# A fused S4D and SwiGLU block on one Trainium2 core: gate and up projections of two token blocks at once by Strassen's scheme

## The chip, the core and the metric

The kernel runs on one NeuronCore of one Trainium2 chip. A core has TensorE (PE, matrix products into PSUM), VectorE (DVE), ScalarE (ACT), GpSimd (POOL) and SyncE (SP), whose queue issues most DMA transfers. The metric is the time of one execution on the device in microseconds, lower is better. Three runs of the kernel before gave 1016.65, 1013.78 and 1016.82 us; the median is 1016.65 us.

## The reference

Input `x` is 2048 tokens of 640 channels. Stage A is a state space convolution, stage B a gated feed-forward layer with a hidden width of 1728:

```python
def _B_ref(x, w1, w3, w2):
    gate = jnp.einsum("bsd,df->bsf", x, w1)
    up = jnp.einsum("bsd,df->bsf", x, w3)
    h = _silu(gate) * up
    out = jnp.einsum("bsf,fd->bsd", h, w2)
    return out
...
h = _layernorm(x, axis=-1) * (1 + ca) + sa
x = x + ga * _A_ref(h, A_log_A_real, A_A_imag, A_C_real, A_C_imag, A_log_dt, A_D_skip)
h = _layernorm(x, axis=-1) * (1 + cb) + sb
x = x + gb * _B_ref(h, B_w1, B_w3, B_w2)
```

The six vectors `sa` to `gb` come from a product of `silu(c)` with `w_mod`. The change is in the second half, the layer norm and `_B_ref`; all operands are float32.

## The kernel before

**Stage A** (up to about 390 us of the span) makes the convolution in five channel blocks of 128 by small products. Its instructions stand in a table of tasks (`Plan`), whose ranks in `RANKS` set the order on every engine; they go through a helper that records them, so most have line 156 in the profile. Its result goes to the DRAM tensor `zd`, from where the last inverse product (`inverse`, matmuls `iy`) reads it row by row as tiles `iz` and adds it to the tokens `x2`. The fifth channel block is finished last, and its part of `zd` is read apart, as `izb`.

**Stage B** (`ffn`) works on four blocks of 512 tokens. A block is normalised (`ln2`): statistics on DVE, `xn` on ACT and DVE, 20 transposes on PE (`tp`), then `v`, split into a high part `xh` and a low part `xl`. Every float32 operand is split so: `split` copies it to a rounded form on ACT (line 658) and subtracts that on DVE (line 659). A float32 product is then three matmuls, high by high, high by low, low by high (lines 769 to 771 in `up`, lines 803 to 805 in `down`).

The hidden width is 13 tiles of 128 and a last one of 64, where gate and up share one tile. For each block and tile, `weights_load` fetches 128 columns of `w1`, `w3` and 128 rows of `w2`, `split` makes `wh`, `wl`, `w2h`, `w2l`; `up` makes gate and up in two PSUM banks with 2 x 5 x 3 = 30 matmuls of 128x512; `gate` makes `a = silu(gate) * up` (tanh on ACT, two operations on DVE) and splits it into `ah` and `al`; `down` adds the tile's part to five banks `acc` with 15 matmuls. `down` of a tile is called behind `up` of the next one, across the border of two blocks too. `output` scales `acc`, transposes it back and adds it to `x2`, which is stored. PSUM holds five `acc` banks and three `gu` banks. The tile framework's scheduler sets the order in stage B, by the program's order and its own estimate.

While block 0 runs, its `mid` reads and inverts rows 4 to 15 of `zd`, two at a time; rows 0 to 3 were done ahead of it. All weights are fetched and split again for each of the four blocks.

Of the kernel before, what the change touches and what calls it, by code (L numbers as in the profile page):

```python
# [18 lines left out]
P = 128  # L19
# [147 lines left out]
class Plan:  # L167
# [7 lines left out]
    def __init__(self, **rings):  # L175
        self.tasks, self.n = {}, rings

    def add(self, name, eng, took, f, after=(), rank=0.0, port=False, take=(), give=(), table=None, dma=None):
        assert name not in self.tasks, name
        take = [(r, name + "".join(x), k) for r, k, *x in take]  # L180
# [86 lines left out]
    def run(self):  # L267
# [3 lines left out]
        assert not found or len(found) == len(T)  # L271
        self.order = self.place(dict(zip(T, found)) if found else {n: t[4] for n, t in T.items()})
# [5 lines left out]
class K:  # L278
# [34 lines left out]
    def rsqrt(self, pool, var, n, tag, mean, scale=1.0, work=None):  # L313
# [3 lines left out]
        y = pool.tile([P, n], F32, name=f"rs_y_{tag}", tag="rs_y")  # L317
        nb = pool.tile([P, n], F32, name=f"rs_n_{tag}", tag="rs_n")
# [16 lines left out]
    def ln_begin(self, pool, tag):  # L335
        return (pool.tile([P, 4, KT, 6], F32, name=f"st_{tag}", tag="ln_st", bufs=1),
                pool.tile([P, 4, 2], F32, name=f"mv_{tag}", tag="ln_mv", bufs=1))
# [302 lines left out]
    def inverse(self, j0, nj, z, ps, tag, bufs, d0, d1):  # L640
        nc = self.nc
        w = d1 - d0
        for j in range(nj):
            for o, n in ((0, w),) if w <= 512 else ((0, 320), (320, 320)):
                py = ps.tile([P, 512], F32, name=f"iy{j0 + j}_{d0 + o}", tag=tag, bufs=bufs)
                for pr in range(2):
                    nc.tensor.matmul(py[pr * 64:(pr + 1) * 64, :n], self.wd[:, j0 + j, pr, :], z[pr][:, j, o:o + n],
# [13 lines left out]
    def ln2(self, b, pool, ps, stats=None, po=None):  # L661

        nc = self.nc
        xs = self.x2[b]
        st, mv = stats or self.ln_begin(pool, f"n{b}")
        for j in range(4):
            self.ln_part(st, xs, j, KT - 1 if stats else 0, KT)
        rstd, nb = self.ln_end(pool, st, mv, f"n{b}")
        xn = pool.tile([P, 4, D], F32, name=f"xn{b}", tag="xn", bufs=1)
        for j in range(4):  # L670
            if j % 2:
                nc.vector.tensor_scalar(xn[:, j, :], xs[:, j, :], rstd[:, j:j + 1], nb[:, j:j + 1], op0=ALU.mult, op1=ALU.add)
            else:
                nc.scalar.activation(xn[:, j, :], xs[:, j, :], AF.Identity, scale=rstd[:, j:j + 1], bias=nb[:, j:j + 1])
        xh = pool.tile([P, KT, 512], F32R, name=f"xh{b}", tag="xh", bufs=2)
        xl = pool.tile([P, KT, 512], F32R, name=f"xl{b}", tag="xl", bufs=2)
# [15 lines left out]
    def weights(self, b, m, wp):  # L692
        return self.weights_load(b, m, wp)()
# [792 lines left out]
```

## Time and profile before

| | us |
|---|---|
| median of three runs | 1016.65 |
| profiled execution, span from first to last instruction | 1015.7 |
| median less that span | 0.95 |
| PE busy in the span | 892.4 |
| DVE, ACT, POOL busy | 655.7, 506.8, 279.5 |

The answers of the trace hold no time of the profiled execution itself beside its span; the 0.95 us are the difference to the median of the other runs. In the profile a matmul's busy time reaches to its modelled end, and the next starts before that, so a group of matmuls shows a mean of 0.39 us where one starts every 0.23 us; how many fall in a stretch tells the rate. "Idle before" is what an engine waited just ahead of a group. Rows that start with SPq are DMA issues of SP's queue.

### The profile page before, as it was taken

The numbers are of one execution on the slowest core, as the hardware profiler recorded it, in microseconds if no ns is written. First come the engines' busy times: TensorE is split into PE (matmuls) and PEld (weight loads), VectorE is DVE, ScalarE is ACT, GpSimd is POOL, SyncE is SP. The second block draws the span as 40 slices with busy tenths as digits, with TensorE's granted clock in tenths as the row PEclk, the third lists the DMA queues.
The fourth block names the chain that finished last, engine by engine and source line by source line (L and its number), as shares of the span: only waits on it lengthen the run. The fifth ranks groups of instructions, "written<-read, shape, count | busy, mean of one in ns | idle before, by whom it ended". The sixth has DMA issues, their size and how long they took to land.

```text
span 1015.7 us, 20252 instructions
## 1 busy us (share of the span) xinstructions
PE 892.4 (88%) x8129; PEld 713.3 (70%) x8129; DVE 655.7 (65%) x1212; ACT 506.8 (50%) x845; POOL 279.5 (28%) x288
## 2 busy tenths in 40 slices
PE   1464878789999884899999999999999999999996
PEld 1133756767887762677788888888888888888884
DVE  7998899989999474677674453463553643534332
ACT  6867788879787540432243342342442432523231
POOL 1798798978998200100000000000000000000000
PEclk9977998989999897899999999999999999999998
DMA  9965453524131759867232353232443323533302
GB/s 216 264 203 165 105 134 104 141 61 109 37 93 47 194 132 238 211 169 170 77 101 81 111 141 112 78 104 78 127 120 109 88 79 100 139 108 91 103 14 53
DMA packets 140998, 122.05 MB, mean 120 GB/s; under 512 B 13416, under 2 KB 124776, under 8 KB 139368
## 3 DMA queue, kind: packets, MB, share of 16 engines
q1 hardware_dynamic: 140360, 120.49, 44.4%
q8 instruction: 64, 1.05, 0.4%
q10 hardware_dynamic: 544, 0.26, 0.1%
q14 instruction: 30, 0.25, 0.1%
HBM read 99.75 MB, written 20.97 MB: 119 GB/s over the span
## 4 chain that ended last, share of the span: by engine, by line
PE 73%; DVE 14%; ACT 4%; issue 3%; DMA 3%; POOL 1%; SPq 1%; ACTq 0%; DVEq 0%
PE gu L770 12%; PE gu L771 12%; PE gu L769 12%; PE acc L803 6%; PE acc L804 6%; PE acc L805 6%; PE ps L156 4%; PE kps L156 3%; DVE yy L156 3%; PE fz L156 3%; PE fk L156 2%; PE fh L156 2%; DVE fp L156 2%; DVE xx L156 2%; DVE hn L156 2%
## 5 line engine op out<-in xcount | busy, mean ns | idle before, releaser
L770 PE MATMUL gu<-xl,wh 128*128 128x512 f32 x540 | 212.1, 393 | 0.0
L771 PE MATMUL gu<-xh,wl 128*128 128x512 f32 x540 | 211.2, 391 | 0.0
L769 PE MATMUL gu<-xh,wh 128*128 128x512 f32 x540 | 210.1, 391 | 0.6 <-ACT xh L658 0.6
L658 ACT ACTIVATE wh<-wr 128x640 fp32r<-128x640 f32 x105 | 71.8, 731 | 137.3 <-PE gu L770 137.3
L726 POOL MEMSET w2l<- 64x640 f32 x3 | 1.9, 629 | 450.4 <-PE acc L804 450.4
L769 PEld LDWEIGHTS gu<-xh,wh 128*128 128x128 f32 x540 | 101.3, 188 | 23.6 <-ACT xh L658 0.8
L770 PEld LDWEIGHTS gu<-xl,wh 128*128 128x128 f32 x540 | 101.5, 188 | 22.1 <-DVE xl L659 0.2
L771 PEld LDWEIGHTS gu<-xh,wl 128*128 128x128 f32 x540 | 101.4, 188 | 21.5
L803 PE MATMUL acc<-ah,w2h 128*128 128x512 f32 x260 | 103.9, 399 | 0.3 <-ACT ah L658 0.3
L804 PE MATMUL acc<-ah,w2l 128*128 128x512 f32 x260 | 102.2, 393 | 0.0
L783 DVE SCALAR_TENSOR_TENSOR a<-th,gu 128x512 f32<-128x512 f32 x52 | 35.8, 688 | 101.2 <-ACT th L782 101.2
L784 DVE TENSOR_TENSOR a<-a,gu 128x512 f32<-128x512 f32 x52 | 35.8, 688 | 99.5 <-PE gu L771 99.5
L782 ACT ACTIVATE th<-gu 128x512 f32<-128x512 f32 x52 | 31.1, 599 | 134.1 <-PE gu L771 134.1
L805 PE MATMUL acc<-al,w2h 128*128 128x512 f32 x260 | 96.5, 392 | 0.0
L156 POOL TENSOR_TENSOR yy<-e,e 128x512 f32<-128x512 f32 x80 | 86.2, 1093 | 19.4 <-PE kps L156 14.6
L659 DVE TENSOR_TENSOR wl<-wr,wh 128x640 fp32r<-128x640 f32 x105 | 82.1, 819 | 10.6 <-ACT wh L658 10.6
L658 ACT ACTIVATE w2h<-w2r 128x640 fp32r<-128x640 f32 x51 | 37.7, 738 | 87.0 <-issue 47.7
L156 POOL TENSOR_TENSOR ph<-p,p 128x1024 int32<-128x1024 int32 x40 | 79.0, 1976 | 7.5 <-ACT tr L156 6.7
L659 DVE TENSOR_TENSOR w2l<-w2r,w2h 128x640 fp32r<-128x640 f32 x51 | 42.0, 824 | 57.7 <-ACT w2h L658 57.4
L156 PE MATMUL kps<-yy,xx 128*32 128x64 f32 x2560 | 51.7, 235 | 30.8 <-DVE xx L156 20.3
L156 DVE TENSOR_TENSOR yy<-yy,tr 128x512 f32<-128x512 f32 (+1 forms) x80 | 75.5, 946 | 0.9 <-ACT tr L156 0.6
L156 PEld LDWEIGHTS kps<-yy,xx 128*32 128x32 f32 x2560 | 45.2, 117 | 40.8 <-issue 24.9
(205 smaller groups left out, 1645.1 us busy)
## 6 DMA issues: line engine op xcount, KB each, us to landing
wr<-in_w SPq DMA_DIRECT2D x104, 320.0 KB, 3.7
w2r<-in_w SPq DMA_DIRECT2D x52, 320.0 KB, 2.9
zd<-zt SPq DMA_DIRECT2D x40, 256.0 KB, 3.0
iz<-zd SPq DMA_DIRECT2D x24, 320.0 KB, 6.9
xs<-in_x SPq DMA_DIRECT2D x16, 320.0 KB, 10.7
hs<-hb SPq DMA_DIRECT2D x20, 256.0 KB, 2.4
xb<-hs SPq DMA_DIRECT2D x20, 256.0 KB, 4.5
x<-in_x SPq DMA_DIRECT2D x16, 320.0 KB, 9.7
```

The lines of the kernel that those rows point to most:

```text
L156: self.prev = self.k.order(f(*a, **kw), self.prev)
L658: self.nc.scalar.activation(H, v, AF.Copy)
L659: eng.tensor_tensor(Lo, v, H.bitcast(F32), op=ALU.subtract)
L769: nc.tensor.matmul(pg, wh[:, k, :], xh[:, k, :], start=(k == 0), stop=False)
L770: nc.tensor.matmul(pg, wh[:, k, :], xl[:, k, :], start=False, stop=False)
L771: nc.tensor.matmul(pg, wl[:, k, :], xh[:, k, :], start=False, stop=(k == KT - 1))
L782: nc.scalar.activation(th, gu[0], AF.Tanh, scale=0.5)
L783: nc.vector.scalar_tensor_tensor(a, th, 1.0, gu[0], op0=ALU.add, op1=ALU.mult)
L784: nc.vector.tensor_mul(a, a, gu[1])
L803: nc.tensor.matmul(acc[k], w2h[:, sl], ah, start=(m == 0), stop=False)
L804: nc.tensor.matmul(acc[k], w2l[:, sl], ah, start=False, stop=False)
L805: nc.tensor.matmul(acc[k], w2h[:, sl], al, start=False, stop=(m == 12))
```

## The change

Token blocks are taken in pairs. For a pair, the contraction over 640 channels is cut in 2 x 256 and a rest of 128. Gate and up by first and second half, times first and second half by two blocks, is a 2x2 by 2x2 product of blocks; `group` makes it with seven products of 128 x 256 x 512 for eight (Winograd's form of Strassen's scheme), each of 2 x 3 matmuls, and adds the rest directly: 7 x 6 + 4 x 3 = 54 matmuls for a tile of a pair. Before, two blocks took 2 x 30.

- `x_sums` makes four sums and differences of the pair's activations (`T1` to `T4`), once for a pair; `factors` makes four of the weights on POOL for each tile; `part(i)` splits the eight operands of the next tile, each into a buffer of its own that is used again right behind the product that read it.
- Bank `x` is read by ACT and then added to, three times a group; ACT copies and DVE adds take the place of direct reads of PSUM.
- Weights `w1` and `w3` are fetched and split for a pair, `w2` for each block.
- The hidden tile of the pair's second block is kept in SBUF (`ha`, `hb`), and its down projection runs behind all the tiles of the pair, in `late`, 205 matmuls in a row. For pair 0, `late` also holds the norm, the transposes and the sums of blocks 2 and 3, and the 64-wide tile of pair 1. For pair 1 the last two tiles go by output column, with `output` between, and the block is stored in two parts.
- Tile 0 and the 64-wide tile of pair 0 and the 64-wide tile of pair 1 go the plain way (`plain`).
- In stage B the matmuls are chained in the order of the program (`InOrder`), so their line is 156.
- Rows 4 to 7 of `zd` and the tokens of block 1 are read ahead of stage B, as four new tasks of the plan with ranks of their own (`own`); rows 8 to 15 are read one at a time in the groups.
- `wd` is four tiles for one, a few small tiles have two buffers, and the descriptor scratch of software DMA is set to 8192 bytes.

```diff
-        def mid(b, m):
-            if b == 0 and m in (1, 3):
-                self.load_x2((m + 3) // 2)
-            if b == 0 and 2 <= m + 1 < 8:
-                self.inverse_unit(m + 1, ip, ps, "gu", 3)
-            if m == 8 and b < 3:
-                nxt[b + 1] = self.ln2(b + 1, pool, ps)
...
-        self.ffn(nxt, wp, pool, ps, po, mid)
...
+    def x_sums(self, X, v, p, i, tag, bufs):
...
+        def one(t, a, b, eng):
+            d = self.tmp(f"{t}{p}{i}", tag, bufs)
+            eng.tensor_tensor(d, a, b, op=ALU.subtract)
+            h, l = X[t]
+            self.split(h[:, i], l[:, i], d, nc.vector)
+            return d
+        t1 = one("T1", v12, v11, nc.vector)
+        t2 = one("T2", v22, t1, nc.vector)
+        one("T4", v21, t2, nc.gpsimd)
+        one("T3", v22, v12, nc.gpsimd)
...
+    def factors(self, p, m, raw):
+
+        nc = self.nc
+        V, G = nc.vector, nc.gpsimd
+        s = [self.fp.tile([P, 2, P], F32, name=f"s{i}{p}_{m}", tag=f"s{i}") for i in range(4)]
+        g, u = raw[:, 0], raw[:, 1]
+
+        def sums():
+            G.tensor_tensor(s[0], u[:, 0:2], u[:, 2:4], op=ALU.add)
+            G.tensor_tensor(s[1], s[0], g[:, 0:2], op=ALU.subtract)
+            G.tensor_tensor(s[2], g[:, 0:2], u[:, 0:2], op=ALU.subtract)
+            G.tensor_tensor(s[3], g[:, 2:4], s[1], op=ALU.subtract)
+        src = {0: g[:, 0:2], 1: g[:, 2:4], 2: s[3], 3: u[:, 2:4], 4: s[0], 5: s[1], 6: s[2], 7: raw[:, :, 4]}
+        W = {}
+
+        def part(i, eng=None):
+            W[i] = self.operand(i, f"{p}{m}", src[i], eng or V)
+        return sums, part, W
...
+    def product(self, out, w, x, start, stop=True):
+        for k in range(2):
+            self.three(out, [t[:, k] for t in w], [t[:, k] for t in x], start and k == 0, stop and k == 1, not start)
+
+    def rest(self, out, W, i, x, more=False):
+        self.three(out, [t[:, i] for t in W[7]], [t[:, 0] for t in x], False, True, more)
...
+    def hidden(self, b, m, th, g, u):
+
+        V, A = self.nc.vector, self.nc.scalar
+        V.scalar_tensor_tensor(g, th, 1.0, g, op0=ALU.add, op1=ALU.mult)
+        if b % 2:
+            h = self.h[m] = self.h_tile(m)
+            V.tensor_mul(h, g, u)
+            return
+        V.tensor_mul(g, g, u)
+        return self.hidden_split(b, m, g, self.nc.vector)
...
+    def group(self, p, m, W, X, step, mid, quick):
...
+        copy = lambda o, i: A.activation(o, i, AF.Copy)
+        tanh = lambda o, i: A.activation(o, i, AF.Tanh, scale=0.5)
+        b11, b21, k40, k41 = X[0, 0], X[0, 1], X[0, 2], X[1, 2]
+        x = self.bank(f"X{n}")
+        self.product(x, W[0], b11, True)
+        g0 = self.tmp(f"g0{n}")
+        copy(g0, x)
+        step(0)
+        c = self.bank(f"c0{n}")
+        self.product(c, W[1], b21, True, False)
+        self.rest(c, W, 0, k40)
+        self.add_(g0, c, g0)
+        t0 = self.tmp(f"t0{n}")
+        tanh(t0, g0)
+        step(1)
+        e = self.bank(f"c1{n}")
+        self.product(e, W[4], X["T1"], True)
+        u1 = self.tmp(f"u1{n}")
+        copy(u1, e)
+        step(4)
+        mid()
+        self.product(x, W[5], X["T2"], False)
+        g1 = self.tmp(f"g1{n}")
+        copy(g1, x)
+        step(5)
+        quick()
+        self.product(e, W[2], X[1, 1], False, False)
+        self.rest(e, W, 0, k41, True)
+        self.add_(g1, e, g1)
+        t1 = self.tmp(f"t1{n}")
+        tanh(t1, g1)
+        step(2)
+        self.product(x, W[6], X["T3"], False)
+        u0 = self.tmp(f"u0{n}")
+        copy(u0, x)
+        step(6)
+        c = self.bank(f"c2{n}")
+        self.product(c, W[3], X["T4"], True, False)
+        self.rest(c, W, 1, k40)
+        self.add_(u0, c, u0)
+        step(3)
+        self.rest(x, W, 1, k41, True)
+        self.add_(u1, x, u1)
+        step(7)
+        a = self.hidden(0, m, t0, g0, u0)
+        self.hidden(1, m, t1, g1, u1)
+        return a
...
+    def ffn(self, cut):
...
+        first, half = self.ahead
+        h0 = self.plain(0, X, [(0, first[0]), (13, half[0])])
+        for b in (2, 3):
+            self.load_x2(b)
+        xn = self.ln_norm(1, *self.ln_stats(1, *self.stats[1], KT - 1))
+        for k in range(KT):
+            v[1, k] = self.tmp(f"v1{k}", "hb", 10)
+            self.turn_x(1, k, xn, X, v[1, k], acc_bank(1, k), k % 2)
+        acc = self.accumulators(0)
+        self.down(acc, 0, h0[0], first[1], True, False)
+        self.plain(1, X, [(0, first[0])])
+        self.down(acc, 13, h0[1], half[1], False, False)
+        raw, w2r = self.up_load(0, 1), self.down_load(0, 1)
+        sums, part, W = self.factors(0, 1, raw)
+        sums()
+        for i in (0, 1, 7, 4, 3):
+            part(i)
+        self.plain(1, X, [(13, half[0])])
+        for i in (5, 2, 6):
+            part(i)
+        for i in range(2):
+            self.x_sums(X, [v[0, i], v[1, i], v[0, 2 + i], v[1, 2 + i]], 0, i, "tmp", 7)
+        w2 = self.down_split(0, 1, w2r)
+        pend = self.groups(0, range(1, 13), X, acc, W, w2, None)
+        acc, X, W, w2, pend = self.late(0, acc, pend)
+        pend = self.groups(1, range(13), X, acc, W, w2, pend)
+        self.late(1, acc, pend)
...
+    def groups(self, p, tiles, X, acc, W, w2, pend):
+
+        for m in tiles:
+            more = m < 12
+            if more:
+                raw, w2r = self.up_load(p, m + 1), self.down_load(2 * p, m + 1)
+                sums, part, W2 = self.factors(p, m + 1, raw)
+                sums()
+            rows = []
+
+            def mid():
+                if pend is not None:
+                    self.down(acc, *pend, False)
+                if p == 0 and m < 9:
+                    rows.append(self.inverse_row(7 + m))
+                    rows[0](0)
+
+            def quick():
+                if rows:
+                    rows[0](320)
+            a = self.group(p, m, W, X, part if more else lambda i: None, mid, quick)
+            pend = (m, a, w2, False)
+            if more:
+                W, w2 = W2, self.down_split(2 * p, m + 1, w2r)
...
+    def late(self, p, acc, pend):
...
+        ready(0)
+        self.down(acc, *pend, True)
+        if p == 0:
+            xn.append(self.ln_norm(2, *self.stats[0]))
+        for k in range(KT):
+            self.output(2 * p, acc, k)
+        self.store(2 * p)
+        acc = self.accumulators(b)
+        for i, m in enumerate(self.H[:n - self.LAST] if p else self.H):
+            a = self.hidden_split(b, m, self.h.pop(m), nc.gpsimd if i % 2 == 0 else nc.vector)
+            self.down(acc, m, a, w2.pop(i), i == 0, i == n - 1)
+            ready(i + 1)
...
+            if i in (6, 8):
+                for k in (0, 2) if i == 6 else (1, 3, 4):
+                    v[1, k] = self.tmp(f"v3{k}", "hb", 10)
+                    self.turn_x(3, k, xn[1], X, v[1, k], self.bank(f"tp3{k}"), False)
+            if i in (7, 9):
+                c = (i - 7) // 2
+                self.x_sums(X, [v[0, c], v[1, c], v[0, 2 + c], v[1, 2 + c]], 1, c, "tmp", 7)
...
+        if p:
+            keep = []
+            for i in range(n - self.LAST, n):
+                keep.append((self.H[i], self.hidden_split(b, self.H[i], self.h.pop(self.H[i]), nc.vector), w2.pop(i)))
+                ready(i + 1)
+            for k in range(KT):
+                for m, a, w in keep:
+                    self.down(acc, m, a, w, False, m == self.H[-1], [k])
+                if k:
+                    self.output(b, acc, k - 1)
+                if k == 3:
+                    self.store(b, 0, 3 * P)
+            self.output(b, acc, KT - 1)
+            self.store(b, 3 * P, D)
+            return None
...
+        a, = self.plain(2, X, [(13, half)])
+        self.plain(3, X, [(13, half)])
...
+        for k in range(KT):
+            self.output(1, acc, k)
+        self.store(1)
+        return self.accumulators(2), X, W, self.down_split(2, 0, w0), (13, a, w13, True)
...
+        done = [f"z{b - 1}.{j}.o{f}" for j in range(4) for f in range(2)]
+        add("fx1", "SP", 0, lambda: self.load_x2(1), ["fx", "iz0", "iz1"], -30, dma=[327680] * 4, own=True)
+        for u in range(4):
+            more = dict(own=True) if u > 1 else {}
+            add(f"iz{u}", "SP", 0, lambda u=u: load_z(u), ["change", "fx"] + done + (["fx1"] if u > 1 else []), W if u < 2 else -25 + u,
...
+        self.pe = InOrder(self, real.tensor)
```

The places that the prediction speaks of, as the two kernels' instructions stand. A name's number only tells buffers apart.

SP's queue at the end of stage A, where the last results go to `zd` and the first reads of stage B start (`x_` are token blocks, `iz` and `izb` reads of `zd`). Before:

```order
L156 DMA zd<-zt_5200 128x4x128
L156 DMA zd<-zt_5203 128x4x128
L637 DMA izb_5222<-zd 64x4x128
L637 DMA izb_5223<-zd 64x4x128
L627 DMA x_5219<-in_x 32x2560 x4
```

After:

```order
L156 DMA zd<-zt_5205 128x4x128
L156 DMA x_4853<-in_x 32x2560 x4
L156 DMA zd<-zt_5235 128x4x128
L156 DMA zd<-zt_5238 128x4x128
L156 DMA iz_5241<-zd 64x2x512 x2
L156 DMA iz_5242<-zd 64x2x512 x2
L156 DMA iz_5247<-zd 64x2x512 x2
L156 DMA iz_5248<-zd 64x2x512 x2
L681 DMA izb_5301<-zd 64x4x128
L681 DMA izb_5302<-zd 64x4x128
```

Twelve transfers now stand ahead of `izb` that stood behind it or later: four of a token block and eight of `iz`.

PE at the end of a token block, where the last hidden tile (12) is projected down. Before, at the end of block 0 (`gu` is gate and up of block 1):

```order
L769 MATMUL gu_01_6513<-xh_6095,wh_0_6502 128x512
L770 MATMUL gu_01_6513<-xl_6096,wh_0_6502 128x512
L771 MATMUL gu_01_6513<-xh_6095,wl_0_6503 128x512
L803 MATMUL acc_5374<-ah_12_6490,w2h_12_6437 128x512
L804 MATMUL acc_5374<-ah_12_6490,w2l_12_6438 128x512
L805 MATMUL acc_5374<-al_12_6491,w2h_12_6437 128x512
```

After, at the end of pair 0's groups (`X_12` is the last product of tile 12 itself):

```order
L156 MATMUL X_12_7560<-x8h_5576,wh_012_7543 128x512
L156 MATMUL X_12_7560<-x8l_5577,wh_012_7543 128x512
L156 MATMUL X_12_7560<-x8h_5576,wl_012_7544 128x512
L156 MATMUL acc_5580<-ah_12_7651,w2h_12_7556 128x512
L156 MATMUL acc_5580<-ah_12_7651,w2l_12_7557 128x512
L156 MATMUL acc_5580<-al_12_7652,w2h_12_7556 128x512
```

Between tile 12's products and its down projection stood 30 matmuls of the next block; now there is none.

DVE in `late` of pair 0, where the down projection of block 1 meets the first sums of pair 1 (`v` comes from transposes, `T` are sums, names in `l` are low parts). These rows are new:

```order
L733 TENSOR_SCALAR v_7989<-tp_7990,cols 128x512
L733 TENSOR_SCALAR v_8000<-tp_8001,cols 128x512
L760 TENSOR_TENSOR T_8044<-v_7989,v_7812 128x512
L662 TENSOR_TENSOR x4l_7997<-v_7989,x4h_7996 128x512
L760 TENSOR_TENSOR T_8048<-v_8000,T_8044 128x512
L662 TENSOR_TENSOR x5l_8008<-v_8000,x5h_8007 128x512
L662 TENSOR_TENSOR x2lT_8037<-T_8044,x2hT_8036 128x512
L662 TENSOR_TENSOR w2l_7_8031<-w2r_7_7987,w2h_7_8030 128x640
```

Seven operations stand ahead of `w2l_7`, which the down projection of tile 7 reads.

More of the change, by code (lines that the diff above doesn't have):

```diff
@@ L663, in ln2, with turn_x @@
+    def turn_x(self, b, k, xn, X, v, where, pool):
         nc = self.nc
-        xs = self.x2[b]
-        st, mv = stats or self.ln_begin(pool, f"n{b}")
         for j in range(4):
[L667 to L674, printed above, removed]
```

414 lines of the change are left out of this document (256 added, 158 removed).

## The prediction

> **What bounds the kernel now.** I read the page first (engines, slices), then stretches of the span, the groups of instructions in stage B, and the timeline at its two ends.
>
> ```profile
> PE 892.4 (88%) x8129; PEld 713.3 (70%) x8129; DVE 655.7 (65%) x1212; ACT 506.8 (50%) x845; POOL 279.5 (28%) x288
> PE   1464878789999884899999999999999999999996
> ```
>
> ```profile
> core 0: us, PE busy (x) PEld busy (x) DVE busy (x) ACT busy (x) POOL busy (x), PEclk, DMA share, GB/s
> 393.20:411.00 17.80, 6.14 (x29) 5.38 (x30) 5.84 (x27) 1.74 (x2) 0.00 (x0) 0.54 1.00 232
> 400.00:425.00 25.00, 17.44 (x80) 13.94 (x80) 13.16 (x37) 10.03 (x15) 2.57 (x2) 0.77 0.96 218
> 412.90:431.60 18.70, 17.41 (x76) 12.00 (x77) 12.20 (x22) 9.08 (x15) 2.57 (x2) 1.00 0.84 205
> 431.60:1003.00 571.40, 571.40 (x2580) 463.43 (x2579) 287.54 (x496) 198.71 (x308) 1.89 (x3) 1.00 0.37 102
> 550.00:575.00 25.00, 25.00 (x111) 20.52 (x110) 9.42 (x13) 6.67 (x11) 0.00 (x0) 1.00 0.35 99
> 1003.00:1015.80 12.80, 3.41 (x22) 2.09 (x20) 3.27 (x5) 2.76 (x5) 0.00 (x0) 0.74 0.44 102
> ```
>
> From 431.6 to 1003 us PE has no gap: 571.4 busy of 571.4, full granted clock, DVE at half, ACT at a third, POOL empty. There a matmul is worth its issue interval, 25.00 / 110 = 0.227 us (the 111th is cut by the stretch's edge). Ahead of it, from 393 to 411, the core waits for DMA: share 1.00 at 232 GB/s. So what the change takes from PE's count is gained, unless it makes PE wait where it never waited.
>
> **The change part by part.** The work it touches, from the groups:
>
> ```profile
> L769 PE MATMUL gu<-xh,wh 128*128 128x512 f32 x525 | 205.1, 391 | 0.0
> L647 PE MATMUL iy<-iz,wd 128*64 128x320 f32 x80 | 12.4, 442 | 0.0
> L659 DVE TENSOR_TENSOR wl<-wr,wh 128x640 fp32r<-128x640 f32 x101 | 78.9, 819 | 10.6 <-ACT wh L658 10.6
> L659 DVE TENSOR_TENSOR w2l<-w2r,w2h 128x640 fp32r<-128x640 f32 x51 | 42.0, 824 | 57.7 <-ACT w2h L658 57.4
> L658 ACT ACTIVATE w2h<-w2r 128x640 fp32r<-128x640 f32 x51 | 37.7, 738 | 87.0 <-issue 47.7 <-PE acc L805 32.2 <-PE acc L808 7.0
> L784 DVE TENSOR_TENSOR a<-a,gu 128x512 f32<-128x512 f32 x51 | 35.1, 688 | 99.5 <-PE gu L771 99.5
> L659 DVE TENSOR_TENSOR al<-a,ah 128x512 fp32r<-128x512 f32 x51 | 34.9, 684 | 2.0 <-ACT ah L658 2.0
> L658 ACT ACTIVATE ah<-a 128x512 fp32r<-128x512 f32 x51 | 31.5, 618 | 7.8 <-DVE a L784 7.8
> L782 ACT ACTIVATE th<-gu 128x512 f32<-128x512 f32 x51 | 30.5, 599 | 130.1 <-PE gu L771 130.1
> L688 DVE TENSOR_SCALAR v<-tp,cols 128x512 f32<-128x512 f32 x15 | 11.9, 807 | 3.4 <-PE tp L683 3.4
> L816 ACT ACTIVATE oc<-acc,cols 128x512 f32<-128x512 f32 x16 | 10.8, 679 | 6.7 <-PE acc L805 4.5 <-PE to L819 2.0
> ```
>
> *Matmuls.* 12 groups of pair 0 and 13 of pair 1 take 54 for 60: 25 x 6 = 150 fewer, all 128x512, in a stretch where PE never idles. 150 x 0.227 = **-34.1 us**. `down`, transposes and the plain tiles keep their count.
>
> *Rows 4 to 7.* 16 matmuls `iy` leave that stretch for the wait ahead of it: 16 x 12.4 / 80 = **-2.5 us**.
>
> *The start.* The rows:
>
> ```profile
> 386.40 3.59 SPq L156 DMA_DIRECT2D zd<-zt  x4
> 391.93 1.25 SPq L637 DMA_DIRECT2D izb<-zd  x2
> 393.23 8.13 SPq L627 DMA_DIRECT2D x<-in_x  x8
> ...
> 401.17 1.94 PE L647 MATMUL iy<-izb,wd 128*64 128x128 f32 x10 [4.31 <-DMA izb<-zd]
> ...
> 412.97 0.97 PE L769 MATMUL gu<-xh,wh 128*128 128x512 f32 x3 [0.59 <-ACT xh L658]
> ```
>
> Stage B starts when `izb` has landed (401.17), 11.8 us ahead of its first product (412.97). SP's order now puts block 1's tokens (4 x 0.328 MB) and eight `iz` (8 x 0.262 MB) ahead of it. From 386.4, zd 1.05 + tokens 1.31 + `iz` 2.10 + `izb` of block 0 0.52 = 4.98 MB at 232 GB/s take 21.5 us: 407.9 for 401.2, **+7 us**. Below: ACT's queue issues half of `izb` and may overtake, +3; above: the second `izb` (2.3 us) and the statistics of block 1 on DVE come first, +12. The 11.8 us behind it hold the same chain. From the first product on, 18.7 us held 76 matmuls where 17.3 would do at 0.227; behind the new start DVE has some 23 us of work (splits, two gates, sums) for 22 us of PE, so I add 0, between -1 and +6.
>
> *Within a group.* With 15 of `down` it is 69 matmuls, 15.7 us. DVE does eight splits of 256 columns (0.684 less 256 x (0.819 - 0.684) / 128 = 0.41 each), four adds and four gate operations at 0.69, `al` and `w2l`: 10.3 us. ACT does four copies and two tanh at 0.60, eight copies of about 0.4, `ah`, `w2h`: 8.2. Both are hidden by PE. The waits are by chain. W5's product adds to bank `x` behind 9 + 6 + 15 matmuls; W6's behind 9 (2.0 us), while ACT needs 0.2 + 0.4 + 0.6 = 1.2 us to copy `x`; the rest's behind 9, with a tanh ahead too, 1.6 of 2.0. The border: the gate needs two adds, a product, `ah`, `al`, with three splits between, about 4 us, ahead of `down` at 21 matmuls or 4.8 us. Margins are 0.4 to 0.8 us, so I take 0.08 us a group, **+2 us**, 0 to 0.6 each.
>
> *The seam at a pair's end.* `down` of tile 12 followed 30 matmuls (6.8 us) of the next block; now nothing is between. Last product to DVE 0.2, add 0.69, product 0.69, `ah` 0.62, hops 0.2: 2.4 us; `al` is later still (a split 0.41 and the other block's gate 0.69 ahead of it), 0.6. Twice 3.0 = **+6 us**. What then is late: five `output` share DVE with `al`, and `down` of tile 13 waits for its own split, 1.3 us each time, **+2.6 us**.
>
> *`late`.* A tile of `down` is 15 x 0.227 = 3.4 us; ACT needs 0.62 + 0.74, then DVE 0.82 for `w2l`: 2.5 us with hops, or 3.3 with POOL's `w2l` (below). Its weights come in time:
>
> ```profile
> w2r<-in_w SPq DMA_DIRECT2D x52, 320.0 KB, 2.9
> ```
>
> The slot is free one split after the tile before last, so issue, 2.9 us and split end about 0.8 us ahead of need. That holds in the plain tiles. With the sums of pair 1, two `v` and five operations (1.6 + 5 x 0.69 = 5.1) stand ahead of `w2l` 0.82: ready 5.9 + 0.8 us after the operand is free, against eight transposes 1.2 + 3.6 of PE. That leaves 1.9 us, twice: **+4 us** (0 to 8). Behind the 64-wide tile, ACT has a tanh and a copy ahead of `oc`, 1.2 + 0.68 + 0.5: **+2.4 us**. In pair 1 the last two tiles need `ah`, `w2h`, `w2l` within 3 matmuls (0.7 us): 2.7 - 0.7 = **+2 us**.
>
> *POOL beside DVE.* Four sums a group and half of `late`'s subtractions go to POOL, empty before.
>
> ```profile
> L156 POOL TENSOR_TENSOR yy<-e,e 128x512 f32<-128x512 f32 x47 | 49.3, 1069 | 6.7 <-PE kps L156 6.7
> ```
>
> ```profile
> 412.95 0.69 DVE L659 TENSOR_TENSOR xl<-v,xh 128x512 fp32r<-128x512 f32 x1 [0.16 <-ACT xh L658]
> 414.00 1.42 DVE L659 TENSOR_TENSOR xl<-v,xh 128x512 fp32r<-128x512 f32 x1 [0.35 <-ACT xh L658]
> 415.52 0.81 DVE L688 TENSOR_SCALAR v<-tp,cols 128x512 f32<-128x512 f32 x1
> ```
>
> ```profile
> 413.58 1.29 POOL L659 TENSOR_TENSOR xl<-v,xh 128x512 fp32r<-128x512 f32 x1 [61.20 <-DMA iz<-zd]
> 415.37 1.29 POOL L659 TENSOR_TENSOR xl<-v,xh 128x512 fp32r<-128x512 f32 x1 [0.51 <-ACT xh L658]
> ```
>
> The same subtraction takes DVE 0.69 us alone and 1.42 us where it starts inside POOL's: POOL ends at 414.87, DVE at 415.42, 0.55 later. It stood still, while `v`, with its input in PSUM, did not beside POOL's second. A sum of 256 columns is at most half of 1.07 plus a start, 0.6 us; four a group can hold DVE 2.4 us, `late`'s POOL work (1.29, and 1.6 for 640 columns) up to 1.3 an operation. DVE has the room (10.3 + 2.4 of 15.7); the margins above do not always. I take **+3 us** in all, from 0 to what rival 2 says.
>
> The Trainium skill (SBUF — State Buffer, "Who interferes with whom") states this as a rule: a DVE operation with two SBUF inputs and a GpSimd operation that reads SBUF exclude each other for a whole instruction. The rows agree; by that rule nearly all of DVE's new splits and gate products can be held, which is rival 2 below.
>
> The skill (TensorE: Matmul & The Clock Gate, "HAM oscillation — how this bites in real kernels") also has PE's clock halve behind some 3.4 us of idling. The 400 to 425 row, with PE's waits and a granted clock of 0.77, agrees; a seam that grew from 3.0 past it would by that page cost some 1.7 us more, and the sum would be 3 us higher.
>
> *The end.*
>
> ```profile
> 1002.11 1.31 PE L805 MATMUL acc<-al,w2h 128*128 128x512 f32 x5
> ...
> 1006.97 0.69 DVE L821 TENSOR_TENSOR x<-to,x 128x512 f32<-128x512 f32 x1 [0.20 <-PE to L819]
> 1007.69 3.37 SPq L823 DMA_DIRECT2D out<-x  x4
> ```
>
> Last matmul 1003.0, last add 1007.7, end 1015.7. Now four of five `output` run between matmuls: `oc` 0.9, transposes 0.7, add 0.8, 2.4 for 4.7; and the last store is 0.52 MB for 1.31, 3.4 us less at 232 GB/s, of which I count 2.7. **-5 us**, between -2 and -6.
>
> *At nothing*: half the weight loads and splits go away where DMA is at 0.35 and DVE at half (hidden by PE's 25.00 of 25.00; uncovered, loads of 0.64 MB a tile would take 2.8 us); `wd` in four tiles is the same bytes; spare buffers and the software DMA scratch touch nothing on the path.
>
> The sum: -34.1 - 2.5 + 7 + 2 + 6 + 2.6 + 4 + 2.4 + 2 + 3 - 5 = -12.6 us. The span 1015.7 becomes 1003.1; the median is 0.95 above it, so **1004 us**.
>
> **The rivals.**
>
> 1. *PE's queue stays full.* The scheduler's order of DVE and ACT covers groups, `late` and POOL; only the start (+7) and the two seams (+6) cost. -34.1 - 2.5 + 7 + 6 - 5 = -28.6: 988 us. For it: DVE and ACT have 5 us to spare in every group. Against: PE's order is fixed now, so one late operand stops all behind it.
> 2. *Slower: each group's hand-over is late.* POOL's sums hold DVE's splits and adds, and DVE's lateness reaches a bank or operand that PE's next row needs. The price is up to 2.4 us a group; if half of it reaches PE, 25 x 1.2 = 30 us for my 2 + 3: 1004 - 5 + 30 = 1029 us. It decides from (12.6 + 5) / 25 = 0.7 us a group on. For it: the 1.42 us row, margins of 0.4 to 0.8 us. Against: a 0.6 us sum meets at most one DVE operation, and sums need no fixed moment.
> 3. *The start swallows it.* Two blocks must be normalised ahead of the first group and DVE is the bound there: the start at its upper bound (+5), the stretch behind it too (+6), and `late`'s sums (+4) make 15 us more, 1019 us at the worst, 1014 at two thirds of it, no change to see. For it: DMA share 1.00. Against: PE has 22 us of plain tiles to bridge.
> 4. *It doesn't do what it says.* PE's rows hold 1470 gate and up matmuls for 1620, and 820 of `down` in both; under 1 in 100.
>
> **How the numbers follow.** 0.3% is 3.05 us, about what a measurement of this kernel can tell from no change. Forecast (994 to 1011): 0.60. Rival 1: 0.19. Rival 3: 0.10. Rival 2: 0.11. Faster: the first two and a third of rival 3, 0.82; within 0.3%: 0.07, most of it rival 3; slower: rival 2, 0.11. The forecast alone spans 994 to 1011; to leave out no more than 2 in 10, the range takes in rival 1's centre and rival 3's: **986 to 1016 us**.
>
> **What would show it.** Right: 150 fewer 128x512 matmuls, 0.227 us apart in the groups; first product of block 0 near 420 us; PE idle some 3 us twice, ahead of the first `acc` behind a pair's last tile; waits of `acc` on DVE in `late` of pair 0; last add about 5 us ahead of the end. Wrong: PE idle of over 0.5 us in every group, released by DVE (rival 2); a start past 425 us; a POOL operation lengthened to 2 us; `late` without gaps (rival 1).

## The result, and the profile after

The changed kernel took 1043.95 us (median of 4 runs, 1041.36 to 1045.95), the kernel before 1016.18 (4 runs, 1013.78 to 1016.82): 1.0285 times as long, 95% interval 1.026 to 1.0309. Slower by 2.9%, where 1004 us was forecast, within 986 to 1016. The profiled execution spans 1041.9 us, 26.2 more than before.

The page of the changed kernel, its engines and two rows of slices:

```profile
PE 883.4 (85%) x7979; PEld 693.5 (67%) x7979; DVE 734.5 (70%) x1400; ACT 576.8 (55%) x1070; POOL 410.2 (39%) x423
PE   1474887798999873879999999997889999999897
PEclk9987999999999897888999999999999999999998
```

PE has its 150 matmuls less (7979 for 8129) and is 9.0 us less busy, but the row of slices that was all 9 behind the start now has dents; the clock's row, in tenths, shows those behind the start too. The stretches follow, with the columns as before. They are cut at the first product, the first group, the second group, the end of pair 0's last product, the first product of pair 1, the end of pair 1's last product and the end of PE's last instruction:

```profile
420.47:454.96 34.49, 31.32 (x138) 25.39 (x136) 20.80 (x29) 17.18 (x31) 6.47 (x5) 0.93 0.25 72
454.96:482.30 27.34, 18.86 (x63) 12.16 (x62) 23.66 (x36) 12.10 (x25) 12.96 (x11) 0.75 0.10 31
482.30:668.83 186.53, 186.53 (x816) 144.03 (x814) 127.56 (x283) 84.85 (x179) 31.08 (x41) 1.00 0.26 75
668.83:765.01 96.18, 77.90 (x330) 59.94 (x331) 54.34 (x69) 45.03 (x75) 30.36 (x22) 0.92 0.28 78
765.01:970.11 205.10, 205.09 (x894) 167.93 (x892) 121.84 (x224) 95.04 (x199) 33.29 (x45) 1.00 0.22 60
970.11:1036.24 66.13, 59.96 (x260) 47.55 (x260) 22.99 (x29) 25.01 (x39) 17.64 (x12) 0.95 0.30 79
```

From the second group on the groups do what they should: PE busy 186.53 of 186.53 and 205.09 of 205.10, full clock, one matmul each 0.229 us. Behind the first product all the loss lies between them: in the plain tiles and the first group, in pair 0's `late`, and in pair 1's. PE's waits from the first product on, by what ended them (us in total, times, longest; the largest groups):

```profile
PE acc L156 <- DVE w2l L662: 6.4, 3, 3.2
PE c L156 <- ACT x6hT L661: 4.9, 1, 4.9
PE acc L156 <- ACT ah L661: 4.4, 3, 2.0
PE acc L156 <- POOL w2l L662: 4.3, 5, 1.1
PE iy L156 <- DVE g L853: 3.5, 1, 3.5
PE to L156 <- ACT oc L989: 3.4, 2, 3.1
PE acc L156 <- DVE ah L880: 3.3, 2, 1.7
```

That is not yet all. PE's timeline at the end of pair 0:

```profile
668.43 0.40 PE L156 MATMUL X<-x8h,wl 128*128 128x512 f32 x1
670.87 0.79 PE L156 MATMUL acc<-ah,w2h 128*128 128x512 f32 x1 [2.04 <-ACT ah L661]
671.46 0.63 PE L156 MATMUL acc<-ah,w2l 128*128 128x512 f32 x1
671.89 0.66 PE L156 MATMUL acc<-al,w2h 128*128 128x512 f32 x1
...
674.05 0.51 PE L156 MATMUL acc<-ah,w2l 128*128 128x512 f32 x1
674.40 0.39 PE L156 MATMUL acc<-al,w2h 128*128 128x512 f32 x1
674.63 0.39 PE L156 MATMUL acc<-ah,w2h 128*128 128x512 f32 x1
```

Behind a wait of 2.04 us the matmuls start 0.43 us apart, not 0.23, for 3.4 us. Such stretches stand behind nine of the ten waits over 1.5 us in this trace: seven of 3.4 us, and one of 13.7 us (462.67 to 476.33) around the two waits of the first group.

The granted clock tells when. In all thirteen traces of this case its changes lie whole multiples of 3.41 us apart, so the span can be cut in windows of that length. Two pairs of them, at pair 0's end and at pair 1's (PE busy, PEclk, DMA share, GB/s):

```profile
667.48:670.89 3.41, 1.37 (x7) 1.00 0.70 192
670.89:674.30 3.41, 3.41 (x8) 0.50 0.67 191
967.84:971.26 3.42, 2.27 (x10) 1.00 0.00 0
971.26:974.67 3.41, 2.52 (x10) 1.00 0.00 0
```

At pair 0's end PE is idle for 2.04 us of one window, and the next is granted half the clock. At pair 1's end the same wait (970.11 to 972.15) is split over two windows, and the clock stays. Counted over every full-clock window of stage B in the thirteen traces: with PE idle under 1.53 us none of 2102 is followed by half the clock, with over 1.85 us 53 of 53, and between the two 11 of 26.

So where the 26.2 us are, worked out from all rows of PE from the first product to its last (a 128x512 matmul at 0.228, an `iy` of 320 columns at 0.157, a transpose at 0.105; what is left over is rows further apart than that): start 420.47 - 412.97 = +7.5; work -39.5; waits 35.7 for 1.7, +34.0; rows further apart 32.3 for 5.2, +27.1, of which 18.9 are the clock (half of it was granted for 42.2 us, and PE was busy in 37.75 of them), about 4 are `iy`, and the rest is in the main the matmul ahead of each wait, which is counted to its end here; PE's last end to the span's end 5.7 for 8.8, -3.1. Sum +26.0.

### The profile page after: what moved, and what is told of

Its sections match the earlier page's. It is cut to its first block, busy times and chain, and to the rows that moved or that the text cites. A ratio compares the mean times of both kernels' runs of the same rounds, so it can differ in the third digit from the quotient of the medians.

```text
span 1041.9 us, 20733 instructions
## 1 busy us (share of the span) xinstructions
PE 883.4 (85%) x7979; PEld 693.5 (67%) x7979; DVE 734.5 (70%) x1400; ACT 576.8 (55%) x1070; POOL 410.2 (39%) x423
## 4 chain that ended last, share of the span: by engine, by line
PE 64%; DVE 18%; DMA 8%; issue 4%; ACT 4%; SPq 1%; POOL 0%; POOLq 0%; DVEq 0%; ACTq 0%
PE c L156 18%; PE acc L156 17%; PE X L156 12%; PE ps L156 4%; DVE yy L156 3%; PE kps L156 2%; PE fk L156 2%; PE fz L156 2%; PE fh L156 2%; DVE xx L156 2%; DVE hn L156 2%; DVE fp L156 2%; DMA sp<-in_w_mod 2%; DMA xs<-in_x 2%; PE iy L156 1%
## 5 line engine op out<-in xcount | busy, mean ns | idle before, releaser
L661 ACT ACTIVATE wh<-wr 128x256 fp32r<-128x256 f32 x100 | 41.7, 418 | 62.6 <-PE X L156 46.9
L156 PEld LDWEIGHTS acc<-ah,w2l 128*128 128x128 f32 x280 | 55.5, 198 | 25.7 <-DVE w2l L662 7.7
L156 PEld LDWEIGHTS acc<-ah,w2h 128*128 128x128 f32 x280 | 55.4, 198 | 24.1 <-ACT ah L661 5.5
L889 ACT ACTIVATE t<-g 128x512 f32<-128x512 f32 x50 | 31.6, 632 | 60.9 <-DVE g L853 60.9
L661 ACT ACTIVATE wh<-s 128x256 fp32r<-128x256 f32 x100 | 41.0, 410 | 43.2 <-PE c L156 20.6
L156 PEld LDWEIGHTS acc<-al,w2h 128*128 128x128 f32 x260 | 50.8, 195 | 15.3 <-DVE al L662 4.1
L662 DVE TENSOR_TENSOR wl<-s,wh 128x256 fp32r<-128x256 f32 x100 | 42.8, 429 | 23.1 <-ACT wh L661 21.0
L858 DVE SCALAR_TENSOR_TENSOR g<-t,g 128x512 f32<-128x512 f32 x50 | 34.6, 693 | 32.4 <-ACT t L889 32.1
L662 DVE TENSOR_TENSOR wl<-wr,wh 128x256 fp32r<-128x256 f32 x100 | 43.8, 439 | 19.2 <-ACT wh L661 19.2
L156 ACT ACTIVATE tr<-ph,hpi 128x512 f32<-128x512 f32 x80 | 54.7, 691 | 3.6 <-DVE xx L156 2.0
```

Of the source, the lines that this page charges most:

```text
L156: self.prev = self.k.order(f(*a, **kw), self.prev)
L661: self.nc.scalar.activation(H, v, AF.Copy)
L662: eng.tensor_tensor(Lo, v, H.bitcast(F32), op=ALU.subtract)
L858: V.scalar_tensor_tensor(g, th, 1.0, g, op0=ALU.add, op1=ALU.mult)
L889: tanh = lambda o, i: A.activation(o, i, AF.Tanh, scale=0.5)
```

## Experiments

Each kernel ran once, under the profiler, and is set beside the change's own profile, except where an interval is given. The table shows the stretches in us (the first product's place; from it to the first `down` of tile 12; pair 0's `late` to pair 1's first product; pair 1's groups to that `down`; the rest to the span's end). In "seam" and "everything" 15 and in "mended" and "`oc`" 9 matmuls of `down`, 3.4 and 2.1 us, stand in the stretch behind.

| kernel | first product | to tile 12's `down` | pair 0's `late` | pair 1's groups | rest | span |
|---|---|---|---|---|---|---|
| the change | 420.5 | 250.4 | 94.1 | 207.1 | 69.8 | 1041.9 |
| slot | 421.1 | 250.7 | 82.4 | 206.5 | 71.3 | 1032.0 |
| late without POOL | 418.8 | 250.2 | 84.4 | 206.9 | 64.8 | 1025.0 |
| sums early | 425.3 | 242.2 | 94.0 | 207.2 | 69.8 | 1038.5 |
| slot and no POOL | 422.3 | 249.4 | 74.4 | 206.5 | 66.3 | 1018.8 |
| seam, `iy` together | 420.4 | 251.3 | 93.7 | 200.9 | 73.0 | 1039.2 |
| start without POOL | 418.6 | 241.7 | 90.5 | 206.5 | 68.0 | 1025.3 |
| everything | 421.2 | 242.9 | 79.5 | 201.9 | 67.8 | 1013.3 |
| cover | 421.2 | 240.2 | 92.1 | 207.2 | 69.8 | 1030.4 |
| `oc`, part of the seam | 419.9 | 246.5 | 92.3 | 203.2 | 68.8 | 1030.7 |
| mended | 420.6 | 233.1 | 73.7 | 203.3 | 66.9 | 997.6 |

The first product's place scatters from 418.8 to 425.3 us over kernels that do the same up to there, so stretches tell more than spans. But a stretch that an edit doesn't touch differs too: that to tile 12 by 1.3 us, pair 0's `late` by 2.0, pair 1's groups by 0.8, the rest by 3.3. Differences of that size need the rows beside them. The theory after the result was: three stretches in which something with its own cause makes PE wait, and the clock on top of each wait. The rival was one cause, POOL's operations holding DVE.

**1. One slot of `w2r`.** The tile `w2r`, into which the rows of `w2` are loaded, has two buffers (slots). The chain of waits of the changed kernel in pair 0's `late`:

```profile
732.39 2.87 DMA w2r<-in_w
...
735.34 0.75 ACT w2h L661
...
736.21 1.58 POOL w2l L662
737.81 2.81 DMA w2r<-in_w
...
740.73 0.75 ACT w2h L661
741.50 0.84 DVE w2l L662
742.35 2.78 DMA w2r<-in_w
```

Each load starts when the subtraction of the tile ahead has ended: one slot, not two. The other one is held by `w13`, which the change loads at the loop's fifth tile and splits behind its end. The edit moves that load to the thirteenth of the loop's fourteen tiles:

```diff
             if i == 4:
                 half = self.whole(13, self.up_load(1, 13))
-                w13 = self.down_load(2, 13)
+            if i == 12 and not p:
+                w13 = self.down_load(2, 13)
```

> The load of pair 1's tile-13 down weights moves from the fifth tile of `late` to its last, so both `w2r` slots stay with the loop. Slot theory: from tile 5 on the loop has one `w2r` slot, load 2.9, `w2h` 0.74 and `w2l` 0.8 to 1.6 us follow one another, and that is why the last gaps of pair 0's `late` (3.25 at 732.4, 0.36 and 1.12 us behind it, with the slow matmuls after each) are there: they go, the stretch from the last group of pair 0 to the first group of pair 1 shortens by 4 to 9 us, span 1033 to 1038. Rival (the sums of pair 1 on DVE and POOL make `w2l` late, the slot does nothing): under 2 us, span 1040 to 1042, and the 3.25 us gap stays.

The stretch fell by 11.8 us, more than either forecast, and the span to 1032.0. In its chain of waits the three loads are gone and PE stands alone:

```profile
727.24 1.68 DVE al L662
728.92 0.04 issue
728.96 11.72 PE acc L156 x43
```

The slot's theory holds. What was left ahead of PE, DVE's `al` at 1.68 us, is the next experiment's matter.

**2. `late` without POOL.** In the changed kernel, the rows of DVE, then of POOL, at the first half of pair 1's sums:

```profile
712.99 0.68 DVE L662 TENSOR_TENSOR x5l<-v,x5h 128x512 fp32r<-128x512 f32 x1
713.59 1.76 DVE L662 TENSOR_TENSOR x2lT<-T,x2hT 128x512 fp32r<-128x512 f32 x1
715.28 1.88 DVE L662 TENSOR_TENSOR w2l<-w2r,w2h 128x640 fp32r<-128x640 f32 x1
717.08 0.68 DVE L662 TENSOR_TENSOR x3lT<-T,x3hT 128x512 fp32r<-128x512 f32 x1
```

```profile
713.15 1.66 POOL L760 TENSOR_TENSOR T<-v,T 128x512 f32<-128x512 f32 x1 [1.83 <-DVE T L760]
714.77 1.71 POOL L760 TENSOR_TENSOR T<-v,v 128x512 f32<-128x512 f32 x1
```

POOL's first ends at 714.81, its second at 716.48; DVE's `x2lT` and `w2l`, begun inside them, end at 715.35 and 717.16, 0.5 to 0.7 us later. The edit:

```diff
-    w2[i] = self.down_split(b, self.H[i], w2r.pop(i), nc.gpsimd if i % 2 else nc.vector)
+    w2[i] = self.down_split(b, self.H[i], w2r.pop(i), nc.vector)
...
-    a = self.hidden_split(b, m, self.h.pop(m), nc.gpsimd if i % 2 == 0 else nc.vector)
+    a = self.hidden_split(b, m, self.h.pop(m), nc.vector)
...
-    one("T4", v21, t2, nc.gpsimd)
-    one("T3", v22, v12, nc.gpsimd)
+    one("T4", v21, t2, nc.vector if p else nc.gpsimd)
+    one("T3", v22, v12, nc.vector if p else nc.gpsimd)
```

> All subtractions of `late` that POOL does (every second `w2l` and `al`, and T3 and T4 of pair 1) go to DVE. Port theory (a POOL operation holds DVE's for its whole length, 1.4 to 1.9 us rows for 0.68 and 0.82): DVE's operations fall back to 0.68 and 0.82 us, the three gaps that POOL's `w2l` ends (0.87, 1.04, 1.12) go and those of 2.77 and 3.25 shorten to 1 to 2: span 1033 to 1038, and the one in pair 1 at 1025.6 (1.11) goes too. Slot theory: the gaps from 728 us on stay, since the load is what is late: span 1038 to 1041. If DVE alone becomes the bound there: slower than 1042.

Span 1025.0: 9.7 us less in pair 0's `late`, 5 less in pair 1's (part of that can be the rest's scatter), more than forecast. The subtractions of `w2l` on DVE in that stretch, first with the change, then without POOL (grouped, mean ns of one behind the busy time):

```profile
L662 DVE TENSOR_TENSOR w2l<-w2r,w2h 128x640 fp32r<-128x640 f32 x7 | 7.5, 1074 | 14.8 <-ACT w2h L661 14.8
```

```profile
L662 DVE TENSOR_TENSOR w2l<-w2r,w2h 128x640 fp32r<-128x640 f32 x14 | 11.5, 823 | 17.1 <-ACT w2h L661 17.1
```

Twice the work at 0.82 us each took DVE from 54.3 to 53.7 us busy: POOL's half had saved it nothing. The Trainium skill (SBUF — State Buffer, "Who interferes with whom") calls the shared ports an exclusive lock; the rows agree, to the whole length of POOL's instruction. One wait of 2.58 us and two of 0.36 from 722 us on stayed; they went with the slot (5).

**3. The sums early.** The first group waits 4.89 and 3.46 us for pair 0's sums and for `g`, behind which DVE is full. T1, T2, T4 written ahead of tile 1's splits:

```diff
         self.plain(1, X, [(0, first[0])])
+        for i in range(2):
+            self.x_sums(X, [v[0, i], v[1, i], v[0, 2 + i], v[1, 2 + i]], 0, i, "tmp", 7, ("T1", "T2", "T4"))
         self.down(acc, 13, h0[1], half[1], False, False)
```

> The sums T1, T2 and T4 of pair 0 are written ahead of the first tile's splits, T3 stays behind. Ramp theory (the first group waits 4.89 and 3.46 us because DVE does the sums last, with POOL's holding it): the 4.89 us gap at 463.4 falls to 0 to 2, the first group ends 3 to 7 us sooner, span 1035 to 1039. Rival (DVE's whole amount of work between 432 and 472 us sets the end of the first group, whatever its order): the gap moves to another operand, under 2 us, span 1040 to 1042.

The stretch to tile 12's `down` fell by 8.2 us, while the start came 4.8 later by its scatter: span 1038.5. The wait of 4.89 us became one of 3.26, ended by DVE's `g`, and the 3.46 one of 0.37. So the wait moved to another operand, as the rival had it, but order alone was worth more than the rival's 2 us.

**4. Matmuls that nobody reads.** This kernel computes the same and adds 34 matmuls into a spare bank:

```diff
         ready(0)
+        self.idle(f"s{p}", pend[2], X0, 9)
         self.down(acc, *pend, True)
```

> At the end of each pair, 9 matmuls that nobody reads (9 x 0.228 = 2.05 us) fill the wait ahead of the pending `down`, and 8 more the wait ahead of tile 13's `down`. Nothing is computed sooner. Clock theory (a wait of 2 us is followed by 3.4 us at half the clock, 7 or 8 matmuls at 0.43 us): the gaps of 2.04 and 1.6 us at both ends close, the half-clock rows behind them go, and the kernel with more work is 3 to 6 us faster: span 1036 to 1039. Rival (the slow rows have another cause, such as DVE's traffic): the rows stay, span 1042 to 1044.

Span 1037.4. The same place, with the work that nobody reads:

```profile
668.02 2.22 PE L156 MATMUL idles<-x6hT,w2h 128*128 128x512 f32 x9
670.23 0.50 PE L156 MATMUL acc<-ah,w2h 128*128 128x512 f32 x1
670.57 0.40 PE L156 MATMUL acc<-ah,w2l 128*128 128x512 f32 x1
671.10 0.50 PE L156 MATMUL acc<-al,w2h 128*128 128x512 f32 x1
```

`down` starts as late as before against the last product, and goes on at full rate from its fourth matmul on. From the first product to pair 1's first it is 2.4 us less, in pair 1 1.1. These times are near the scatter, but the rows show it: with PE kept busy the half-rate stretches at both seams are gone, so the clock behind a seam is a loss of its own.

**5. Slot and DVE together.**

> The slot of the first experiment and `late` without POOL of the second together. The two acted on the same stretch (pair 0's `late`, 94.1 us with the change, 82.4 with the slot alone, 84.4 without POOL alone; its matmuls at full rate are 65.5). If they are two causes that each hold `w2l` up, what is left is what both left: the two waits at the seam, `oc` and one of pair 1's sums, 73 to 78 us there, and pair 1's end as without POOL, span 1013 to 1019. If they were two ways of relieving one cause, 80 to 82 us there: span 1021 to 1024.

74.4 us and a span of 1018.8, as two causes would have it. Of pair 0's `late` 4.6 us of waits remain, 3.06 of them for `oc`.

**6. PE's order at the seam, and `iy`.**

```diff
+            if not more:
+                mid(True)
...
                     rows[0](0)
+                    rows[0](320)
```

> PE's order alone, the work is the same. In each pair's last group `down` of tile 11 stands behind the group's products, not in their middle: 15 matmuls (3.4 us) that fill the wait for tile 12's hand-over. And both `iy` of a row stand one behind the other. Seam: the 2.04 us waits go, at both pairs' ends, and half-clock rows behind them: -4 to -8 us in all (-4.5 with the matmuls that nobody reads). `iy`: each block of four between 128x512 matmuls costs some 0.25 us beside its own time, eight blocks fewer: -1 to -2.5 us. Span 1032 to 1037. If the clock falls for another reason: -4 from the waits alone, 1036 to 1038.

Span 1039.2, a miss. From pair 1's first product on 3.0 us went, no more than scatter can be, and in pair 0 the rows of `iy` took the gain back in every group:

```profile
492.70 0.76 PE L156 MATMUL iy<-iz,wd 128*64 128x320 f32 x4
494.08 0.76 PE L156 MATMUL iy<-iz,wd 128*64 128x320 f32 x4 [0.62 <-DVE x L706]
```

The second half needs a bank that DVE frees only after the first half's sum: three banks, two in use by the group. The change's place for it, one product later, was right. All of `down` moved also took the cover from `u`'s copy (0.67 us).

**7. The start without POOL.** Beside the sums early, the subtractions of `xl` go to DVE, and T3 and T4 of both pairs.

> The sums early as in the third experiment, and nothing on POOL ahead of the first group but the tiles' own sums: the subtractions of `xl` and T3, T4 of pair 0 go to DVE. Port theory: `al` (1.50 for 0.69) and the `xl` and T rows (1.6 to 1.8) fall back, the 2.87 us wait of the first `down` shortens to 1 to 2 and the first group's 3.6 us that were left go to 0 to 2: plain tiles and first group together 46 to 50 us (61.8 with the change, 53.6 with the sums early), span 1028 to 1035, less or more by what the start's own scatter (418.8 to 425.3 us) does. Rival: DVE is the bound there, so that 1.3 us of POOL's rows become 0.68 more on DVE's path: 53 to 57 us together.

Plain tiles and first group 53.2 us (53.6 with the sums early): the rival's number. POOL's holding was not what kept the first group, DVE's amount of work was. The span of 1025.3 owes 8.7 us to the stretch up to tile 12, most of it the sums' order, 3.7 to pair 0's `late`, where T3 and T4 of pair 1 left POOL, and 1.9 to an early start.

**8. All edits together.** Slot, `late` without POOL, sums early and on DVE, the sixth's order of PE, and block 1's output between the two 64-wide tiles.

> All edits that took time off in their own stretch together: the slot, `late` without POOL, sums early and on DVE, `down` of tile 11 behind the last group's products, both `iy` together, and the outputs of block 1 between the two 64-wide tiles (PE's wait of 3.06 us for `oc` goes). If each loss sits where the trace put it, they add up: -20 in pair 0's `late` with the slot and DVE, -5 in pair 1's, -8 to -14 ahead of the second group, -5 at the seams, -2 `iy`, -3 `oc`: 1044 becomes 998 to 1004, faster than the kernel before by over 1%. If the gaps share causes (DVE full, once POOL is relieved): 1006 to 1014, no better than before.

1015.3 us (10 runs), before 1014.6 (13): ratio 1.0004, 0.9988 to 1.0021, no difference. Both forecasts missed, the rival's 1006 to 1014 by little. The losses of the sixth experiment came along, and `oc` was set behind the 64-wide tile's hand-over on ACT: PE waited 4.71 us for it, where it had been 3.06.

**9. Cover for the sums.** Tile 1 of pair 0 is plain too, and its 60 matmuls stand between the sums and the first group.

```diff
+        self.plain(1, X, [(1, w1)])
+        a1, = self.plain(0, X, [(1, w1)])
...
-        pend = self.groups(0, range(1, 13), X, acc, W, w2, None)
+        pend = self.groups(0, range(2, 13), X, acc, W, w2, (1, a1, w21, False))
```

> Only the start of pair 0: the sums early as in the third experiment and tile 1 plain for both blocks. If the first group was late because DVE's sums and splits had too little of PE's work beside them (order alone left 3.6 us of waits and 2.5 of slow matmuls), the first group runs at full rate and ends, counted from the first product, 54 to 57 us less its own 13.7 + 15.7, that is the stretch from the first product to the second Strassen group takes 64 to 67 us, where the same tiles take 69.3 with the sums early: span 1033 to 1037. If it was one late operand whatever the cover: 69 to 72 us, no gain over the sums early.

67.4 us from the first product to the second Strassen group, just outside the 64 to 67, as the plain tiles still waited 3.5. The first group itself took 17.6 us without a wait, where it took 27.3 with the change: what it lacked was PE's work beside DVE's.

**10. `oc` and part of the seam.**

```diff
+        oc = [self.scaled(1, acc, k) for k in range(KT)]
         a, = self.plain(2, X, [(13, half)])
+        for k in range(KT):
+            self.output(1, acc, k, oc[k])
...
+            if not more:
+                self.down(acc, *pend, False, range(2, KT))
```

> Two edits in stretches apart. `oc` of block 1 ahead of the 64-wide tiles on ACT, its transposes between them: the 3.06 us wait at pair 0's end goes, with the half-clock rows behind it, -3 to -5 us between the last `down` of block 1 and pair 1's first group. In both last groups 9 of tile 11's 15 `down` matmuls stand at the end: both 2.04 us waits go, no wait of `c` on `u` comes, and where the half-clock rows go too, -4 to -7. Together span 1030 to 1035.

Span 1030.7: both waits of 2.04 are gone, and those of `to` at pair 0's end fell from 3.5 to 1.3.

**11. Mended.** Slot, `late` without POOL, sums early and on DVE, tile 1 plain, 9 of 15 matmuls at the seam, `oc` ahead of the tanh, `iy` as the change has it.

> The kernel with all edits, mended where they missed: the `iy` blocks apart again (together they waited 0.62 us a group for a bank); in the last group three fifths of tile 11's `down` behind the products and two fifths in the middle, where all of it away left `u`'s copy 0.7 to 0.8 us late; `oc` of block 1 written on ACT ahead of the 64-wide tile's tanh, not behind its hand-over (4.7 us wait); and tile 1 of pair 0 plain, 60 matmuls for 54 (+1.4 us), so that the sums of pair 0 have 13.7 us more of PE's work to stand beside. From the 1015.3 us of all edits: -3.5 `iy`, -1 `u`, -4 `oc`, -7 first group and + 1.4: 999 to 1004, over 1% faster than before. Rival (with PE fuller, DVE sets the pace in the stretch up to the second group): 1006 to 1012.

999.2 us (4 runs, 998.26 to 1002.45), before 1015.8 (7 runs): 0.9846, interval 0.9826 to 0.9867. It is 1.5% faster than the kernel before and 4.3% faster than the change. Its stretches from the first product on:

```profile
420.56:466.58 46.02, 43.57 (x198) 35.30 (x196) 31.98 (x54) 24.71 (x45) 4.15 (x4) 0.99 0.20 58
466.58:485.19 18.61, 17.88 (x79) 13.12 (x78) 13.43 (x29) 8.67 (x20) 2.96 (x4) 1.00 0.31 88
485.19:653.69 168.50, 168.50 (x739) 129.56 (x737) 117.98 (x264) 76.30 (x161) 27.30 (x36) 1.00 0.27 75
653.69:727.40 73.71, 70.65 (x340) 56.76 (x339) 54.30 (x84) 44.62 (x74) 2.01 (x3) 1.00 0.39 112
727.40:930.68 203.28, 202.36 (x884) 165.75 (x883) 123.25 (x226) 95.75 (x201) 35.25 (x47) 1.00 0.21 57
930.68:992.00 61.32, 59.03 (x270) 46.76 (x268) 29.13 (x42) 25.86 (x40) 0.63 (x1) 1.00 0.32 90
```

The clock reads 0.99 to 1.00 in every stretch.

## Why the prediction was wrong

*Held.* There are 150 matmuls fewer, 0.228 us apart. The start is at 420.47 for "near 420" (+7.5 for +7), but so close a match is partly luck, as the same start scatters by 6.5 us. No wait stands inside the groups, so +2 and the groups' share of +3 were nothing, and rival 2 fell, though POOL's sums of weights took 0.76 us each, where 0.6 was the most that was forecast. The seams' waits, 2.04 + 0.57 + 1.63 and 2.04 + 0.57 + 1.67, are 8.5 us for 8.6; here the first part was shorter than its 3.0 and the second longer than its 1.3, so that the sum is luck too. The end gave 3.1 us for 5. The `iy` rows that moved were 32 records, not 16 (5.0 us for 2.5), and the 64 that stayed, now in blocks of four, cost 0.225 each ((17.6 - 15.8) / 8 from the periods of a group with and without them) for 0.16 in blocks of 12 to 16 before: 4 us given back.

*"Its weights come in time", the step that failed first.* The sentence took two slots for granted "in the plain tiles" and charged only the sums, 1.9 us twice. The two causes that it left out are priced, each with the clock behind its waits: `w13` in one slot, 11.8 us, and POOL's holding DVE, 9.7 us, both together 19.7, all in pair 0's `late`; POOL cost 3.5 to 5 us more in pair 1's. The prediction's +3 us for POOL beside DVE was short of that. Of the sums' own "+4" one wait of 0.37 us was then left, and `oc` had 3.06 for "+2.4". The place was known, `late` of pair 0; what stood in the slot was in the code (a load at tile 5, its split behind tile 13) and was not followed to its release.

*"Behind the new start ... I add 0".* Measured +17.4 us over the plain tiles and the first group: 11.5 us of waits for 1.2, 8.4 of rows further apart for 1.3. The term set 23 us of DVE's work against 22 of PE's. Measured, PE's rows ahead of the first group are 28.3 us at full rate, and DVE was busy 29.2 us from the first product to the end of the longest wait (463.44). So the two do balance, but the sums come last on DVE and the first group needs them first: 8.2 us went with their order alone, and beside more of PE's work (9) the group didn't wait at all. That is rival 3's mechanism, DVE as the bound ahead of the first group, at three times its price of 6.

*The clock.* The prediction put it in no term, and set its only price from a wait past 3.4 us on. Here waits of 1.63 and 2.04 us were followed by half-rate stretches. All of them together cost 18.9 us, some seven tenths of the whole result. The Trainium skill (TensorE: Matmul & The Clock Gate, "HAM oscillation — how this bites in real kernels") has the gate fall behind waits of over some 3.4 us. Here half of that was enough, 1.54 us and more within one window, and the measurement decides. The seams were mis-sized by this: three such stretches, some 5 us, beside waits that were forecast.

*The range.* Each rival took one of these mechanisms with the rest as forecast. Rival 2's 1029 us was nearest in number, but by a price in each group, and no group waited. Rival 3 was nearest in mechanism, but its upper bounds were worked out one operand at a time; the slot and the clock were in none.

## What to carry to other kernels

Where a change fills an engine that never waited with shorter work, the gain survives only in the steady part; look first at its borders, and follow each buffer there from its load to the instruction that frees it. Work given to POOL beside a busy DVE was no relief here: moving it back cost DVE nothing and freed both. And a wait of PE that leaves it idle over some 1.5 to 1.85 us of one 3.41 us window is to be counted with 1.7 us more for the clock, as nearly all waits from 1.6 us on were here, so that filling it, even with a plain tile of six matmuls more, pays.

## What was not expected of the hardware

Half-rate stretches of 3.4 us began behind waits as short as 1.63 us (680.93), and one behind waits of 0.43 and 1.11 close together (1025.62), while waits of 1.04 and 1.12 alone (724.86, 747.65) and even one of 2.04 (972.15) were followed by none. Idle time within one window of 3.41 us sorts them, as counted above; what decides between 1.53 and 1.85 us stays open. `iy` blocks of four among 128x512 matmuls cost 0.06 us a matmul more than in blocks of 12 to 16; putting two blocks together met the bank instead, so the cause wasn't separated. What makes the start scatter between 418.8 and 425.3 us stays open too.
